# A hand-written engine order for an mLSTM layer and two gated MLPs: five loads and sigmoids of the output gates, and a new order of the first third

## The chip, the cores and the metric

The kernel runs on one core of one Trainium2 chip. The metric is the device time of one execution in microseconds (us), the median of several runs. The chip's engines work side by side and each in its own order: the tensor engine (PE), the vector engine (DVE), the scalar engine (ACT), GpSimd (POOL), and SP, whose queue issues nearly all the transfers (DMAs) here.

## The reference, cut to what matters

Inputs are q, k, v of 2 batches, 8 heads, 768 steps, 40 channels; an input, a forget and an output gate; and the weights of two MLPs of 320 x 1536, stored as 64-bit floats.

```python
m_new  = maximum(f + m, i);  f_stab = exp(f + m - m_new);  i_stab = exp(i - m_new)
C = f_stab * C + i_stab * outer(v_t, k_t);   n = f_stab * n + i_stab * k_t
y_t = sigmoid(o_t) * (C @ q_t) / maximum(abs(n @ q_t), 1)
x = y as (1536 tokens, 320)
x = (sigmoid(x @ w_gate) * (x @ w_val)) @ w_out
out = ((x @ w_a) * (x @ w_b)) @ w_out2
```

## The kernel before, in words

The recurrence is computed in 12 chunks of 64 steps, s = 0 to 11. Both MLPs work on 24 weight columns of 128 hidden channels (W0 to W11 of the first, W12 to W23 of the second), cut into units u = 0 to 83. Units 0 to 23 take two token blocks at a time (256 columns), the later ones four (512 columns).

What each engine does, and when, is written out by hand in PLAN (lines 67 to 127): a list of task names, in one order for all engines. Every engine takes its own tasks in the order of the list; a suffix :V, :G or :A says that the task goes to DVE, POOL or ACT. A suffix *n puts n matmuls of zeros (`fill`, line 171, which the profile shows as `first<-zb`) ahead of the task on PE. The tasks that the texts name, by chunk s, half p, gate chunk i, weight column c or unit u:

- `start`, `gl`i: loads of the gates (three chunks of 128, 320 and 320 steps). `ga`, `gb`, `gd`, `gc`i on DVE and `ge`i on ACT (lines 281 to 312) make the row V of cumulated gates from them. `cst` loads constants; `rhs`, `lhs`i copy them.
- `pr`s (line 341) puts V into the operands of `E`ps (PE, line 369), whose exponential `X`ps (ACT, line 378) is the decay matrix Dt. For s of 6 and more `pl`i does it with ten small DMAs.
- `kq`s, `kv`s load q, k and v. `yz`, `yi`i prepare the three buffers of v. `S`s (PE, lines 401 and 416) is k times q, `P`ps (DVE, line 426) multiplies it by Dt, `k`ps and `q`ps (lines 381 and 391) scale k and q by it. `ST`s (PE, line 435) and `st`s (ACT, line 457) update the state, `O`s (PE, line 445) makes the output.
- `og`i loads output gates (line 329, for the chunks named in OGS) and `sg`i takes their sigmoid on ACT (line 339). `N`s, `M`s, `D`s normalise; `T`s (PE) transposes; `xh`s (ACT, line 491) and `xl`s (DVE, line 494) write the high and low half of the MLP's input.
- `w`c loads a weight column (960 KB). `na`c (ACT, lines 218 and 219), `nb`, `ns`, `nc`c (DVE) and `nd`c (DVE, or POOL at about double the duration) narrow 64-bit floats to 32; `s1`c (ACT), `s2`, `s3`c (DVE or POOL) split them into two halves.
- `ma`u, `mb`u (PE, line 524) are a unit's first two products, `ga_`u (ACT), `gp`, `gm`u (DVE), `gh_`u (ACT), `gl_`u (DVE or POOL) its gate, and `mm`u (PE, lines 531 to 533) the product with w_out; `ev` adds it up.

ACT evaluates a function from a table that must be the one loaded. For u below 24 the gate is built of Exp, Tanh and Abs (line 535), which share the table of the Exp in `X`; the output gates' Sigmoid needs another one. The program starts with a Sigmoid on two elements (line 198).

```python
OGS = ((0, 2, 3), (2, 6, 3), (6, 12, 4))      # first chunk, last chunk + 1, weight buffer used
for entry in PLAN.split():
    ...
    if n and first is not None:
        fill(first, int(n))
    fn(eng.get(e))
```

Of the kernel before, what the change touches and what calls it, by code (L numbers as in the profile page):

```python
# [77 lines left out]
M5:V k06:G ma6 P07 gh_4 nb4 gl_4:G mb6 O6 ev1.3:A ga_5 P17 ns4 M4:V ev1.2:A k16:V ST6 gp5 gm5 nc4 ma7 D4 T4
ga_6 D5 T5 gh_5 q17:V gp6 gm6 gl_5:G mm4 xh4 xl4 mb7 xh5 xl5 mm5 ga_7 gh_6 nd4:G gp7 ev2.0 N6 s14 k07:G E08
X08 gl_6:G kq8 k17:V gm7 ma8 M6:V st6 w5 mb8 E18 X18 gh_7 ma9 kv8 gl_7:G E19 mb9 ga_8 q18:G ev2.1 mm6 mm7  # L80
q07:V O7 na5 kq9 gp8 ST7 S8 gm8 ga_9 ma10 mb10 ev3.3 ev3.2 N7 M7:V q08:G kv9 D7 nb5 gp9 ma11 gm9 gh_8 X19 E09
P18 gh_9 gl_9:V kv10 mb11 gl_8:G ga_10 gp10 mm8 st7 pl5 k18:G X09 D6 P08 T6 gm10 gh_10 T7 ns5 xh7 xh6 nc5
k08:G mm9 kq10 k19:V ga_11 xl6 O8 gp11 xl7 ST8 gm11 st8 S9 gl_10:G q19:G nd5:V N8 ma12 mm10 gh_11 E110 X110
mb12 ga_12 ma13 mb13 P09 k09:G s34:V P19 gp12 kq11 s15 gm12 gh_12 gl_11:V ga_13 M8:V ma14 s24:V gp13 D8 q09:G
E010 X010 O9 N9 M9:V gm13 ST9 mb14 s25:V mm11 gl_12:G ga_14 ev4.4:A ma15 gp14 gm14 D9 ev4.5:V gh_13 T8 xh8 xl8
T9 mb15 gl_13:G xh9 xl9 mm12 E111 ga_15 X111 q110:V gh_14 w6 ma16 k110:V gl_14:V mm13 mb16 gp15 gm15 ma17
k010:G mm14 na6 nb6 ga_16 E011 ns6 gp16 gh_15 mb17 nc6 ma18 st9 gl_15:V gm16 ga_17 s35:G w7 kv11 X011 nd6:V
gh_16 s16 mm15 gl_16:G S10 q111:G gp17 gm17 gh_17 S11 q010:V P010 ST10 st10 mb18 ga_18 P110 P111 q011:V P011
ev5.6:V gl_17:G O10 ev5.7:A O11 N10 M10:G mm16 mm17 N11 M11:V na7 D10 D11 T10 T11 gp18 gm18 xh10 gh_18 k111:G
nb7 xh11 xl11 xl10 ma19 mb19 ga_19 gp19 gl_18:G mm18 ns7 ma20 gm19 gh_19 mb20 ga_20 gp20 gm20 gh_20 s36:G ma21  # L90
gl_19:G nc7 mb21 ga_21 gp21 gm21 mm19 ma22 gl_20:G s26:V w8 mb22 ev6.8:A nd7:V ma23 ev6.9:A mm20 mb23 ga_22
gp22 gm22 gh_21 gl_21:G ga_23 gp23 ma24 gm23 s17 mm21 gh_22 mb24 gl_22:G gh_23 gl_23:G ga_24 s27:G k011:V mm22
na8 gm24 ma25 ma26 mb25 s37:G mm23 ga_25 w9 gh_24 mb26 ev7.11:V ev7.10:V gl_24 nb8 ga_26 ma27 ns8 nc8 mm24
gm25 nd8:V gh_25 mb27 gm26 gl_25 ga_27 mm25 na9 ma28 gh_26 gl_26 ma29 gm27 gh_27 ga_28 gl_27 mm26 nb9 ga_29
s18 ns9 nc9 mb28 nd9:V mm27 s38:V s19 s28:V ma30 w10 s29:G ev8.1 gm28 gh_28 mb29 gl_28 ev8.0 ga_30 s39:V ma31
w11 gm29 gh_29 gl_29 ma32 ev8.3 ga_31 na10 mb30 mb31 gm30 nb10 ev8.2 ma33 ns10 nc10 mm28 nd10:G mm29 gh_30
na11 gl_30 gm31 mm30 gh_31 ga_32 gl_31 mb32 s110 mm31 s210:G mb33 s310:G ev9.5 ev9.7 gm32 w12 ev9.4 gh_32 ma34
ga_33 gm33 gl_32 mb34 ev9.6 ga_34 nb11 gh_33 ns11 ma35 nc11 nd11:V mm32 s111 ma36 s211:V s311:G mb35 gl_33
ga_35 w13 mm33 gm35 gh_35 na12 gl_35 ma37 gm34 gh_34 mb36 gl_34 ga_36 mb37 ga_37 gm36 mm34 gm37 ma38 mm35 ma39
gh_36 ev10.11 gh_37 gl_36 ev10.9 ga_38 mb39 ev10.8 gl_37 ev10.10 ga_39 nb12 mb38 ns12 mm36 gm38 gm39 nc12 ma40  # L100
nd12:V mb40 na13 mm37 gh_38 nb13 ns13 ma41 gl_38 gh_39 s112 gl_39 nc13 mm38 ga_40 nd13:G ga_41 mm39 s312:G
mb41 ev11.0 gm40 ev11.1 s212:V ma42 gm41 w14 gh_41 mb42 gh_40 gl_40 gl_41 ga_42 ma43 gm42 ev11.2 ev11.3 yt1
# [831 lines left out]
```

## Time and profile before

| what | value |
|---|---|
| time, median of 3 runs | 476.27 us (474.78 to 476.99) |
| span of the profiled execution | 478.0 us; the page gives no other time for that execution |
| PE busy | 465.6 us, 97% of the span |
| DVE, ACT, POOL busy | 295.1, 242.5, 101.3 us |
| chain that ended last | PE 86%, DVE 6%, ACT 4%, DMA 2% |
| HBM read | 36.71 MB |
| loads, KB each | gates 64 and 160 (twice), cst 469, og 320, 640 and 960, kv twice 162, kq 512 |

The page's slices show PE full from end to end, DVE and ACT full in the first third and half idle later. Busy shares of PE are to be read with care here, since the matmuls of zeros count as busy, and so does a matmul at half the clock.

### The profile page before, as it was taken

The numbers are of one execution on the slowest core, as the hardware profiler recorded it, in microseconds if no ns is written. First come the engines' busy times: TensorE is split into PE (matmuls) and PEld (weight loads), VectorE is DVE, ScalarE is ACT, GpSimd is POOL, SyncE is SP. The second block draws the span as 40 slices with busy tenths as digits, with TensorE's granted clock in tenths as the row PEclk, the third lists the DMA queues.
The fourth block names the chain that finished last, engine by engine and source line by source line (L and its number), as shares of the span: only waits on it lengthen the run. The fifth ranks groups of instructions, "written<-read, shape, count | busy, mean of one in ns | idle before, by whom it ended". The sixth has DMA issues, their size and how long they took to land.

```text
span 478.0 us, 8676 instructions
## 1 busy us (share of the span) xinstructions
PE 465.6 (97%) x3511; PEld 406.2 (85%) x3516; DVE 295.1 (62%) x505; ACT 242.5 (51%) x455; POOL 101.3 (21%) x110
## 2 busy tenths in 40 slices
...
GB/s 226 309 201 240 86 180 224 32 103 183 1 84 84 1 166 0 83 84 1 33 49 84 7 160 0 1 82 138 28 84 82 1 83 1 0 1 20 36 55 55
DMA packets 10454, 39.31 MB, mean 82 GB/s; under 512 B 1840, under 2 KB 3760, under 8 KB 10416
## 3 DMA queue, kind: packets, MB, share of 16 engines
...
q8 instruction: 27, 0.44, 0.4%
...
HBM read 36.71 MB, written 1.97 MB: 81 GB/s over the span
## 4 chain that ended last, share of the span: by engine, by line
PE 86%; DVE 6%; ACT 4%; DMA 2%; issue 2%; SPq 0%; DVEq 0%
PE pa L524 30%; PE pb L524 23%; PE acc L531 8%; PE acc L532 8%; PE acc L533 8%; PE o L445 2%; PE sp L416 2%; DMA wst<-in_w_dram 2%; PE st L435 1%; ACT Dt L378 1%; PE e L371 1%; PE t L487 1%; DVE g L556 1%; PE tp L487 1%; PE first L174 1%
## 5 line engine op out<-in xcount | busy, mean ns | idle before, releaser
L524 PE MATMUL pa<-xb,W 128*128 128x512 f32 (+1 forms) x864 | 169.4, 343 | 0.3 <-DVE ge L605 0.3
L524 PEld LDWEIGHTS pa<-xb,W 128*128 128x128 f32 x864 | 136.3, 188 | 18.9 <-DVE ge L605 0.5
L524 PE MATMUL pb<-xb,W 128*128 128x512 f32 x480 | 119.0, 392 | 0.0
L524 PEld LDWEIGHTS pb<-xb,W 128*128 128x128 f32 x480 | 89.0, 188 | 17.9
L560 ACT ACTIVATE gh<-g 128x512 fp32r<-128x512 f32 (+1 forms) x84 | 47.5, 568 | 110.7 <-PE acc L532 55.6
L531 PE MATMUL acc<-W,gh 128*128 128x320 f32 x288 | 89.3, 310 | 0.0
L532 PE MATMUL acc<-W,gh 128*128 128x320 f32 x288 | 88.9, 309 | 0.0
L533 PE MATMUL acc<-W,gl 128*128 128x320 f32 x288 | 88.8, 309 | 0.0
L554 DVE TENSOR_TENSOR g<-g,pb 128x512 f32<-128x512 f32 x60 | 40.9, 685 | 69.7 <-PE pb L524 61.6
L565 DVE TENSOR_TENSOR gl<-g,gh 128x512 fp32r<-128x512 f32 (+1 forms) x66 | 45.5, 694 | 44.0 <-ACT gh L560 43.8
L549 ACT ACTIVATE g<-pa 128x512 f32<-128x512 f32 x60 | 35.6, 595 | 45.8 <-DVE gl L565 38.1
L532 PEld LDWEIGHTS acc<-W,gh 128*128 128x128 f32 x288 | 54.0, 188 | 2.1
L531 PEld LDWEIGHTS acc<-W,gh 128*128 128x128 f32 x288 | 54.0, 188 | 2.0
L533 PEld LDWEIGHTS acc<-W,gl 128*128 128x128 f32 x288 | 54.0, 188 | 0.0
L258 POOL TENSOR_TENSOR W<-wst,W 128x832 fp32r<-128x832 f32 x9 | 19.1, 2124 | 84.5 <-DVE x2tok L639 42.2
L639 DVE SCALAR_TENSOR_TENSOR x2tok<-acc,x2tok 128x320 f32<-128x320 f32 x52 | 23.8, 485 | 19.5 <-PE acc L533 19.5
L242 POOL TENSOR_TENSOR wst<-cva,wst 128x960 int32<-128x960 int32 x7 | 16.9, 2410 | 73.8 <-DVE cva L236 61.1
L218 ACT ACTIVATE cva<-wst 128x960 f32<-128x960 f32 x24 | 25.8, 1077 | 10.6 <-DVE wst L242 8.8
L252 ACT ACTIVATE W<-wst 128x832 fp32r<-128x832 f32 x24 | 23.2, 966 | 11.5 <-DVE wst L242 8.5
L236 DVE SCALAR_TENSOR_TENSOR cva<-wst,cva 128x960 int32<-128x960 int32 x24 | 27.9, 1161 | 0.4
L565 POOL TENSOR_TENSOR gl<-g,gh 128x256 fp32r<-128x256 f32 x18 | 15.7, 876 | 54.7 <-ACT gh L560 47.3
L219 ACT ACTIVATE wst<-wst 128x960 int32<-128x960 uint32 x24 | 26.1, 1087 | 0.0
...
## 6 DMA issues: line engine op xcount, KB each, us to landing
wst<-in_w_dram SPq DMA_DIRECT2D x24, 960.0 KB
...
og<-in_ogate_dram SPq DMA_DIRECT2D x1, 960.0 KB
...
rhsE<-V SPq DMA_DIRECT2D x24, 2.0 KB
```

The lines of the kernel that those rows point to most:

```text
L218: nc.scalar.activation(cva[0], hi.bitcast(F32), AF.Abs)
L219: nc.scalar.activation(lo, lo.bitcast(U32), AF.Copy, scale=2.0**-29)
L236: nc.vector.scalar_tensor_tensor(ai, hi, -0x40000000, ai, op0=ALU.bitwise_and, op1=ALU.bitwise_or)
L524: nc.tensor.matmul(dst, w[:, w0 : w0 + P], x[:, h, cb], start=(i == 0), stop=(i == 7))
L531: nc.tensor.matmul(a, gh[:, c], wh, start=st, stop=False)
L532: nc.tensor.matmul(a, gh[:, c], wl, start=False, stop=False)
L533: nc.tensor.matmul(a, gl[:, c], wh, start=False, stop=sp)
L549: nc.scalar.activation(t, pa, AF.Copy if l else AF.Sigmoid)
L554: nc.vector.tensor_tensor(t, t, pb, op=ALU.mult)
L560: nc.scalar.activation(gh, g, AF.Copy)
L565: eng.tensor_tensor(gl, g, gh.bitcast(F32), op=ALU.subtract)
L639: nc.vector.scalar_tensor_tensor(dst[:, 0:DM], acc, half, dst[:, 0:DM], op0=ALU.mult, op1=ALU.add)
```

## The change: what it does

Output gates come in five loads (chunks 0-1, 2-3, 4-5 into one buffer, 6-8, 9-11 into another) with five sigmoids. PLAN gets a new order up to the task `gl_21`; its last 682 entries are the same as before. The same tasks are on PE ahead of unit 24 as before. 64 matmuls of zeros become 33, and the 37 ahead of the first E become 2. Some 50 tasks change between DVE and POOL, and two evacuations between ACT and DVE. The load of W0 is issued after that of kq0, and its narrowing starts behind the first two exponentials.

```diff
-OGS = ((0, 2, 3), (2, 6, 3), (6, 12, 4))
+OGS = ((0, 2, 3), (2, 4, 3), (4, 6, 3), (6, 9, 4), (9, 12, 4))
...
-start gl1 cst rhs0:A lhs0:A ga0 ga1 gb0 gd0 ge0 lhs1:A w0 gb1 na0 gc0 gd1 ge1 pr0:V E00*37 og0 X00 rhs1:A
-pr1:V nb0 yz0 kv0 E01*1 E10*6 gl2 gc1 yz2 ns0 yz1 kv1 X01 X10 ga2 pr2:V yi0:A nc0 k10:V kq0 yi2:A k00:V E11*4
-X11 S0 pr3:V w1 kq1 E02 kq2 nd0:V E12 P10 P00 yi1:A k01:G kv2 ST0 st0 na1 X02 og2 S1*10 X12 k11:G k12:G og1
-kq3 gb2 gd2 O0 kv3 ST1 P11 P01 S2*2 pr4:V sg0 nb1 E03 s10 N0 O1*2 P02 P12 st1 s30:G k02:G kq4 ST2 sg2 N1 s20:V
-w2 E13 ns1 sg1 M0:G M1:V X03 nc1 k03:G D1 X13 k13:G O2*1 S3 P03 E04 P13 nd1:V E14 D0 kv4 X04 T0*1 X14 T1 st2
-xh0 N2 S4 ST3 xl0 pr5:G kq5 P14 xh1 kv5 xl1 O3 s11 s31:G s21:V P04 E15 ma0 N3 M2:V na2 mb0 k04:V ge2 ma1 M3:V
-ga_0 mb1 X15 S5 gp0 D3 k14:G st3 nb2 gm0 D2 T2 T3 ga_1 xh2 ns2 gc2 ST4 gh_0 gl_0:G nc2 xh3 O4 st4 kq6 xl2 xl3
...
+yz2 yz0 start ga0 gl1 gb0 ga1 cst gl2 gd0 ga2 lhs1:A rhs0:A ge0 og0 gc0 gb2 lhs0:A kq0 pr0:V w0 E10*2 rhs1:A
+sg0 yz1 gd2 gb1 X10 pr1:V kv0 E00 X00 S0*6 kq1 E11*2 gd1 E01*3 yi0:A k10:G P00 P10 kv1 na0 k00:G ST0*3 ge1 w1
+kq2 X11 X01 yi1:A nb0 st0 yi2:A gc1 ns0 pr2:V O0*1 ge2 nc0 S1 pr3:V kv2 nd0:V E12*3 E02 P11 P01 X02 X12 E13*8
+kq3 N0 gc2 S2 og2 k02:V k01:G k11:G kv3 og1 kq4 s10 pr4:V M0:V P12 og4 s30:G P02 X13 na1 kq5 O1*2 k12:G E04 N1
+nb1 E03 D0 X04 X03 ST1 st1 S3 T0*2 ST2 sg1 M1:V ns1 kv4 k03:G O2 k13:G P03 s20:V w2 nc1 P13 pl3 nd1:V st2 D1
+sg2 xh0 T1*1 N2 xl0 O3 S4 xh1 sg4 s11 E14 xl1 N3 pr5:G ST3 M2:G ma0 X14 k04:G P04 E15 s31:V s21:V P14 na2 mb0
+kv5 E05 X15 ga_0 M3:V D3 X05 D2 k14:V w3 nb2 ma1 ns2 S5 E16 X16 nc2 gp0 st3 nd2:V mb1 T2 kq6 T3 xh2 xl2 xh3
...
+gp3 gm3 gl_2:V M5:V S7 S6 k06:V q07:V P06 kv7 s13 st5 P16 mb4 P17 ST6 og3 na4 D5 mm2
+ga_4 gh_3 T5 s23:G s33:V sg3 xh5 ma5 gp4 gm4 nb4 O6 pl4 ma6 k07:V gh_4 gl_3:V mb5 M4:G st6 D4 mm3 ga_5 q17:G
...
-        ogw[k] = wpool.tile([P, 2 * NH + 2 * P], F32, tag=f"W{k}", name=f"og{k}"), s0
+        ogw[k] = wpool.tile([P, 2 * NH + 2 * P], F32, tag=f"W{k}", name=f"og{k}"), min(o[0] for o in OGS if o[2] == k)
```

## Rows read from the trace of the kernel before

**Rows 1.** Windows by stage: length, busy us of PE, PEld, DVE, ACT, POOL, PEclk, DMA share, GB/s.
```profile
7.00:27.50 20.50, 17.00 (x205) 9.51 (x205) 18.95 (x36) 18.19 (x30) 3.14 (x3) 1.00 1.03 316
27.50:37.60 10.10, 9.35 (x125) 6.88 (x129) 4.68 (x13) 6.78 (x9) 3.31 (x6) 0.50 0.39 98
45.40:103.04 57.64, 56.61 (x808) 53.62 (x806) 52.95 (x102) 47.13 (x111) 23.80 (x24) 1.00 0.43 137
103.04:139.86 36.82, 36.82 (x460) 35.91 (x460) 31.41 (x61) 26.45 (x68) 12.91 (x17) 1.00 0.23 75
139.86:474.00 334.14, 332.75 (x1736) 291.99 (x1734) 177.07 (x273) 135.68 (x225) 51.14 (x49) 1.00 0.15 51
```

**Rows 2.** Timeline of ACT: start, length, line, what, idle before it.
```profile
10.38 1.08 ACT L218 ACTIVATE cva<-wst 128x960 f32<-128x960 f32 x1 [1.66 <-DMA wst<-in_w_dram]
14.71 0.60 ACT L378 ACTIVATE Dt<-e 128x512 f32<-128x512 f32 x1
15.20 1.05 ACT L682 ACTIVATE rhsE<-cs 128x1024 fp32r<-128x1024 f32 x1
...
24.04 1.09 ACT L378 ACTIVATE Dt<-e 128x512 f32<-128x512 f32 x2
25.14 1.28 ACT L339 ACT_TABLE_LOAD   x1
26.44 0.74 ACT L339 ACTIVATE x2tok<-og 128x640 f32<-128x640 f32 x1
```

**Rows 3.** Timeline of PE, matmuls of zeros in two windows, and the first E.
```profile
1.17 5.73 PE L174 MATMUL first<-zb 128*128 128x512 bf16 x13 [1.17 <-DVE zb L178]
7.32 4.70 PE L174 MATMUL first<-zb 128*128 128x512 bf16 x21
11.88 0.58 PE L371 MATMUL e<-rhsE,lhsE 128*128 128x512 f32 x1
```

**Rows 4.** Chain that ended last, in order of time: start, us, what.
```profile
26.02 1.49 issue
...
29.11 0.31 PE sp L401
...
31.52 0.72 PE e L371
...
33.12 1.87 PE o L445 x32
34.99 1.09 PE st L435 x32
...
45.56 3.77 PE pa L524 x32
49.33 0.21 PE sp L401
...
50.69 0.81 PE tp L487 x6
51.50 0.74 PE st L435 x32
52.24 0.93 PE o L445 x32
53.17 0.43 PE e L371
```

**Rows 5.** One window from the first gate load to the second `xl`, columns as in Rows 1.
```profile
3.31:44.65 41.34, 36.55 (x497) 23.28 (x502) 32.25 (x65) 31.02 (x51) 9.99 (x14) 0.88 0.87 261
```

**Rows 6.** Timeline of DVE, the end of `pr0` and the second `xl`.
```profile
10.77 0.28 DVE L351 TENSOR_TENSOR lhsE<-V,cs 32x128 fp32r<-32x128 f32 x1
...
44.10 0.55 DVE L494 TENSOR_TENSOR xb<-tp,xb 128x384 fp32r<-128x384 f32 x1
```

**Rows 7.** The page's DMA issues: KB each.
```profile
wst<-in_w_dram SPq DMA_DIRECT2D x24, 960.0 KB
```

**Rows 8.** Timeline of SP, eight of the ten issues of `pl3`.
```profile
50.60 5.72 SPq L364 DMA_DIRECT2D rhsE<-V  x8
```

More of the change, by code (lines that the diff above doesn't have):

```diff
@@ L73 @@
-xh0 N2 S4 ST3 xl0 pr5:G kq5 P14 xh1 kv5 xl1 O3 s11 s31:G s21:V P04 E15 ma0 N3 M2:V na2 mb0 k04:V ge2 ma1 M3:V
-ga_0 mb1 X15 S5 gp0 D3 k14:G st3 nb2 gm0 D2 T2 T3 ga_1 xh2 ns2 gc2 ST4 gh_0 gl_0:G nc2 xh3 O4 st4 kq6 xl2 xl3
-nd2:V w3 E05 X05 ma2 mb2 s12 gp1 gm1 pl3 ga_2 ma3 P15 P05 gh_1 k05:G na3 mb3 s22:V gl_1:V s32:V mm0 mm1 kq7
-gp2 ma4 mb4 E06 E07 w4 gm2 ga_3 ev0.0:A ev0.1:A nb3 ns3 nc3 nd3:V X06 gh_2 k15:G X07 N4 kv6 S6 gp3 gm3 kv7 E16
-s13 P06 ST5 gl_2:G X16 P16 gh_3 gl_3:V O5 pl4 ga_4 S7 st5 E17 mm2 s23:V s33:G gp4 gm4 N5 mm3 X17 ma5 mb5 na4
@@ L78 @@
[L78 to L102, printed above, removed]
@@ L103 @@
-ma44 yh1 ga_43 yl1 na14 mm40 nb14 mm41 ns14 nc14 yt0 mb43 nd14:V yh0 gh_42 s113 yl0 gl_42 ma45 gm43 ga_44
-s213:G s114 mm42 gh_43 s313:V gl_43 mb45 w15 ga_45 mb44 gm45 mm43 gm44 gh_44 yt3 yt2 ev12.4 ma46 yh3 yh2 yl3
-gh_45 yl2 na15 gl_44 mb46 gl_45 ev12.6 ga_46 ma47 gm46 nb15 s314:V mb47 ns15 ga_47 nc15 ma48 ev12.5 nd15:V
+yz2 yz0 start ga0 gl1 gb0 ga1 cst gl2 gd0 ga2 lhs1:A rhs0:A ge0 og0 gc0 gb2 lhs0:A kq0 pr0:V w0 E10*2 rhs1:A
+sg0 yz1 gd2 gb1 X10 pr1:V kv0 E00 X00 S0*6 kq1 E11*2 gd1 E01*3 yi0:A k10:G P00 P10 kv1 na0 k00:G ST0*3 ge1 w1
@@ new lines @@
+ST4 xl3 O4 ma2 E06 E17 gm0 s12 k05:V kq7 mb2 ga_1 gh_0 P05 P15 k15:G st4 na3 gp1 ma3 gm1 gl_0:V gh_1 N4 nb3
+ga_2 O5 kq9 X06 ST5 gl_1:V X17 mm0 mb3 ns3 gp2 gm2 E07 gh_2 ga_3 mm1 nc3 nd3:V s22:G kv6 ev0.1:A ev0.0:A gp3
+N5 s32:G w4 k16:G ma4 X07 gm3 gl_2:V M5:V S7 S6 k06:V q07:V P06 kv7 s13 st5 P16 mb4 P17 ST6 og3 na4 D5 mm2
+ga_4 gh_3 T5 s23:G s33:V sg3 xh5 ma5 gp4 gm4 nb4 O6 pl4 ma6 k07:V gh_4 gl_3:V mb5 M4:G st6 D4 mm3 ga_5 q17:G
+mb6 P07 T4 ns4 xl5 gl_4:V nc4 ev1.2:V E18 gp5 O7 k17:V ev1.3:A xh4 xl4 gm5 mm4 nd4:V N6 ma7 E08 X18 ga_6 gp6
@@ new lines @@
+X08 gh_5 E19 kq8 gm6 X19 mb7 gl_5:V ga_7 gh_6 M6:V S8 gl_6:G w5 kv8 q19:V P18 mm5 N7 gp7 D6 na5 gm7 M7:G ev2.1
+P08 ma8 T6 mb8 ga_8 xh6 kv9 ev2.0 ma9 gp8 xl6 ST7 E09 mb9 X09 gh_7 gl_7:G mm6 S9 D7 s14 gm8 k18:G ga_9 gh_8
+st7 q18:V ma10 nb5 T7 xh7 k08:G P19 kq10 q08:V mm7 ST8 ev3.2 xl7 gp9 P09 k09:V gm9 ev3.3 pl5 s24:V st8 q09:G
+O8 gl_8:G mb10 E011 N8 ga_10 gp10 kq11 gh_9 mm8 s34:G kv10 gm10 ma11 E010 gl_9:G k19:G O9 X011 M8:G gh_10 N9
+ns5 M9:V X010 gl_10:V mb11 E110 E111 ga_11 D8 gp11 nc5 mm9 ma12 X111 X110 w6 ST9 mb12 q110:V gm11 nd5:V S10
@@ new lines @@
+ma13 P010 ga_12 kv11 D9 gh_11 gp12 k110:G P110 gm12 k010:V q010:G q011:G gl_11:G st9 na6 mm10 T9 T8 ma14 mb13
+ST10 gh_12 gl_12:G ga_13 gp13 xh8 mm11 xh9 mb14 ma15 xl9 gm13 nb6 gh_13 gl_13:G xl8 ev4.5:V ga_14 ev4.4:A s15
+O10 ns6 gp14 N10 mb15 mm12 ma16 nc6 gm14 gh_14 s35:V gl_14:G ga_15 nd6:V q111:G S11 mm13 gp15 mb16 st10 ma17
+mm14 gm15 M10:V ga_16 D10 T10 P011 P111 gh_15 gl_15:G gp16 gm16 s25:V mb17 xh10 gh_16 ga_17 s16 O11 N11 ma18
+gl_16:V M11:V k111:V mm15 mb18 gp17 D11 gm17 ev5.7:A ev5.6:A ma19 T11 w7 xl10 mm16 ga_18 gp18 xh11 gm18 xl11
@@ new lines @@
+gh_17 gh_18 gl_17:G mb19 ga_19 s26:G gp19 gl_18:V na7 s36:V ma20 mm17 mb20 gm19 ma21 mm18 ga_20 gh_19 mb21
+gp20 ma22 nb7 gm20 w8 gl_19:V mm19 gh_20 ns7 gl_20:V ga_21 gp21 gm21 mb22 nc7 ma23 gh_21 ev6.8:A ev6.9:A ga_22
+gp22 mm20 gm22 nd7:V mb23 gl_21:G ga_23 gp23 ma24 gm23 s17 mm21 gh_22 mb24 gl_22:G gh_23 gl_23:G ga_24 s27:G
+k011:V mm22 na8 gm24 ma25 ma26 mb25 s37:G mm23 ga_25 w9 gh_24 mb26 ev7.11:V ev7.10:V gl_24 nb8 ga_26 ma27 ns8
+nc8 mm24 gm25 nd8:V gh_25 mb27 gm26 gl_25 ga_27 mm25 na9 ma28 gh_26 gl_26 ma29 gm27 gh_27 ga_28 gl_27 mm26 nb9
```

11 lines of the change are left out of this document (added).

## The prediction, made before the changed kernel was run

> **What bounds the kernel now.** I first read the windows by stage. From the first product of unit 0 at 45.4 us, PE is idle for 1.0 of 57.6 us, then for none of 36.8, then for 1.4 of 334 us, at the full clock (1.00, which is 2.4 GHz) [rows 1]. The change leaves the work and the order behind unit 24 alone. So the end comes earlier only as far as the start of unit 0 (`ma0`, at 45.56 in the chain [rows 4]) comes earlier and the stage behind it stays as dense.
>
> Second, what sets 45.4. Up to the second `xl`, in the 41.3 us from 3.31 on, DVE is busy for 32.25 us [rows 5]. It waits most between 27.5 and 37.6 us: 4.68 of 10.10 us busy, with PE at a granted clock of 0.50, its 1.2 GHz level [rows 1]. There the chain of waits runs along PE: an idle stretch of 1.49 us at 26.0, then S, O and ST at the lower level [rows 4]. At its start the timeline of ACT shows the other delay. ACT waits 1.66 us for W0, narrows it, and evaluates the first exponential only at 14.71, although its E was issued at 11.88 [rows 2, 3]. So PE and DVE bound the first 45 us in turns, and the later stages are PE's.
>
> **Part 1: W0 after kq0, its narrowing behind X10 and X00.** ACT's old order put the narrowing of W0 ahead of X00. In the new one ACT has, from the 8.72 us at which it went idle [rows 2], one `rhs` copy (1.05 us), the first sigmoid (0.74) and a table load (1.28), which ends at 11.8 [rows 2]. DVE swaps `gb1` and `gd1` ahead of pr0 for `ga2` and `gb2`, about equal work, so pr0 ends at 11.05 as before [rows 6]. Two E at the lower clock (0.72 each [rows 4]) make X10 start at 11.8 and X00 end at 13.0, where X00 alone ended at 15.3 and X10 came after it. kq0 becomes the sixth load; gates, constants, og0 and kq0 are 1685 KB, as much as stood up to W0 before (1653 KB), and W0 was there at 10.38 [rows 2]. W0 and its 960 KB [rows 7] now end 992 KB further on, at 316 GB/s [rows 1] 3.1 us later, at 13.5. ACT reaches it at about 13.9, behind the copy `yi0`, so the later landing costs nothing. If that cover is gone, ge1 and X11 wait as long as W0 is late. On SP nothing is queued behind the later W0 but kv0 and kq1, which have over 3 us to spare. Behind kq3, which waits until P00 and P10 have read kq0 (about 19 us), stand og2, kv3, og1 and kq4, all needed after 25 us. `pl3`, whose first eight issues took 5.72 us [rows 8], now stands ahead of kv5 and w3 on SP; both are wanted some 10 us later, and w3 waits for the split of W1 behind unit 0 anyway. k00 and k10 go to POOL, which was busy for 3.1 of 20.5 us [rows 1], and are done before PE comes to ST0.
>
> **Part 2: zeros, 64 to 33.** Thirteen zeros took 5.73 us from a cold start (0.44 us each), 21 later ones 4.70 (0.22) [rows 3]: the engine had run 5.7 us of back-to-back zeros before the spacing halved. Taking away 35 ahead of the first E frees no time, since X00 waited for ACT. It has a price: E10 now finds PE at the lower level. From 11.0 us on PE has up to `ma0`: 31 zeros, 10 E, 5 S, 4 ST, 4 O, two T. At the full clock these are 31 x 0.22 + 10 x 0.43 + 5 x 1.36 (the S from 49.33 to 50.69) + 4 x 0.74 + 4 x 0.93 + 0.81 = 25.4 us [rows 3, 4]. At the lower one they are 31 x 0.44 + 10 x 0.72 + 5 x 2.41 (29.11 to 31.52) + 4 x 1.09 + 4 x 1.87 + 1.6 (estimated as twice 0.81) = 46.4 us [rows 3, 4]. With H us spent at the lower level PE is ready for `ma0` at 11.0 + 25.4 + 0.453 x H. H is not shown by any row; its bounds are 0 and the whole stretch. I take 6.5, the E, the six zeros and S0 from 11.0 to 17.5, near the 5.7 of the zeros: PE is ready at 39.3.
>
> **Part 3: DVE's order.** Up to the second `xl` the new list has gc2, k02 and M0 more and k00, k10 and P14 less, a wash within 0.3 us, so DVE's work stays 32.2 us. Without any wait it would end at 35.5, with all of the old waits at 44.6. At the share of the stretch from 7 to 27.5 (18.95 of 20.50 [rows 1]) it takes 34.8 us and ends at 38.1. S0, which P00 needs, ends at 17.5, 1.7 us after DVE has come to P00 at about 15.8; added in full that gives 39.8. I take the middle, 39.0. `ma0` stood 0.75 us behind the end of that `xl` (45.40 against 44.65 [rows 6]), so it starts at 39.75, behind PE's 39.3. **Gain: 45.4 - 39.75 = 5.65 us**, between 0 and 9.0 (36.4, PE without any lower clock).
>
> **Part 4: sigmoids and table loads.** The first sigmoid finds its table loaded by the program's start, but the others now come in two batches, `sg1` `sg2` `sg4` and, after unit 0, `sg3`. Each batch needs a load of the Sigmoid's table and one back. After `xh1` ACT now has sg4 (about 1.0 us, from 0.74 for two chunks), a table load (1.28) and X14 (0.6) ahead of the first `ga_`, less ge2 (1.0), which is done before. Around there ACT has no idle to hide them, so this delays the first gate by 1.9 us. sg3 and its two table loads (about 3.6 us) fall into the stage where ACT is busy 47.1 of 57.6 us [rows 1]; 52 of 57.6 still fit. The added DVE work of the moves (about +1.4 us net by this trace's durations, 52.95 of 57.64 busy before) fits too. I take 1.9 us as given back, between 0 (PE has E15, E05, ma1, S5 and E16 to go on with) and 5.5, all of it exposed. The extra og loads cost SP two issues and move no more bytes.
>
> One rule of the Trainium skill speaks against this part. The row first: X's pair ends at 25.13, the table load starts at 25.14 and lasts 1.28, the sigmoid starts at 26.44 [rows 2], so 1.28 is all that the switch cost here. The Trainium skill (ScalarE: Activation LUTs, "What ACT_TABLE_LOAD costs") states 1.28 us for the load and another 1.38 us for emptying the engine, 2.66 in all. By that figure the first gate would be late by 3.3 instead of 1.9 us.
>
> **Sum:** -5.65 + 1.9 = -3.75 us. The profiled execution's 478.0 us, 1.7 above the median, becomes 474.25; put on the median of 476.27 it is **472.5 us**. About 0.5% (2.4 us) is what a measurement can tell from no change.
>
> **The rivals.**
> - *ACT and DVE give it all back.* Unit 0 starts earlier, but the stage behind it, where DVE is 92% busy and ACT rises from 82 to 90%, stretches by the 5.5 us of the bound. For it: the chain runs through DVE and ACT there. Against it: both start that stage earlier as well, with the same work done. 476.27 - 5.65 + 5.5 = 476.1. Chance 0.22.
> - *The cold clock decides.* Without the early zeros PE stays at 1.2 GHz, or falls back in a gap, as at 26 us after an idle of 1.49 us [rows 4]. The place is S0 to S2. The gain is gone when `ma0` reaches 43.5, at H = 15.7, and from H = 21 the kernel is slower by over 0.5%. At H = 30 `ma0` is at 50.0, and the time is 476.27 + 4.6 + 1.9 = 482.8. For it: between 27.5 and 37.6 PE was 93% busy and still got only 0.50 [rows 1]. Against it: zeros stand ahead of S0, E11, E01 and ST0 one after the other. Chance 0.13. The Trainium skill (TensorE: Matmul & The Clock Gate, "What's actually happening") says that throttled is the default and that activity releases it; by that rule the first E of the new kernel run at half rate, and the zeros of the kernel before agree.
> - *Each switch of table also drains ACT.* ACT would then stop for 1.4 us more at a table load (an estimate from the Trainium skill's page named above); with 1.4 us more ahead of the first gate and two more switches for sg3, 0 to 2.8 exposed, the gain shrinks to 2.35 or less: 473.9 to 476.7. The row shows no such stop. Chance 0.03.
> - *The change does not bite:* kq0 or og0 lands late, ACT stands as long as it stood for W0, X10 begins after 14.7 as X00 did. Then the front keeps its 45.4: 476.3. Chance 0.02.
>
> **How the numbers follow.** My case has 0.60: faster by over 0.5% in 0.58 and within it in 0.02. Its own range is 467.3 (9.0 us gained, nothing given back) to 473.8 (H of 10.1, as long as the stretch at 0.50 was: `ma0` at 41.0). The gate stage adds 0.20 to no change and 0.02 to slower; the clock 0.02 and 0.11; the last two 0.05 to no change. So faster 0.58, same 0.29, slower 0.13. The range runs from 467.5 up to 478.5, which is the front's gain gone with the 1.9 us still paid (478.2); beyond it lies only most of the clock's case and the end of the best one.
>
> **What would show it.** Right: X10 at about 12 us; the first S near 15 to 17, with a granted rate of half until about 17 and full from then to 39; DVE idle for under 5 us between 3.3 and the second `xl`; `ma0` between 38.5 and 41; four table loads by `ga_0` and two around sg3; later stages as dense as now, and unit 24 some 4 us before 139.9. Wrong: `ma0` later than 43.5; a stretch at 0.50 of over 16 us in all; PE idle for more than 3 us between unit 0 and unit 24, with ACT or DVE as releaser; X10 still waiting for a load.

## The result, and the profile after

The changed kernel takes 481.3 us (median of 6 runs, 479.87 to 482.08) against 476.88 us of the kernel before beside it (6 runs, 474.78 to 479.58). The ratio is 1.0102, with a 95% interval of 1.007 to 1.0135: about 1% slower. The forecast was 472.5 us and faster, so size and sign both failed.

First the windows by stage of the kernel after (columns as in [rows 1]).

```profile
7.00:27.50 20.50, 15.43 (x203) 9.22 (x207) 19.57 (x36) 19.03 (x33) 5.32 (x7) 1.00 1.03 314
27.50:39.00 11.50, 8.75 (x210) 6.94 (x211) 11.46 (x19) 9.24 (x16) 5.40 (x5) 0.99 0.58 187
39.00:45.60 6.60, 6.58 (x80) 5.69 (x79) 5.78 (x16) 4.83 (x7) 1.66 (x3) 0.50 0.25 85
43.32:145.15 101.83, 99.51 (x1284) 93.99 (x1281) 86.01 (x167) 79.79 (x187) 35.26 (x35) 0.99 0.37 119
145.15:476.00 330.85, 330.04 (x1722) 289.59 (x1720) 175.85 (x270) 133.24 (x219) 51.22 (x49) 1.00 0.15 49
3.31:40.45 37.14, 25.63 (x441) 17.61 (x447) 35.44 (x66) 29.62 (x51) 12.16 (x14) 0.98 0.88 270
```

`ma0` starts at 43.32, and unit 24's second product (the first `pb` of 512 columns, where the order is the old one again) at 145.15. So the stage between them takes 101.83 us. From 27.50 to 39.00 DVE is busy for 11.46 of 11.50 us and PE for only 8.75. The clock is full where it was at 0.50 before [rows 1], and at 0.50 later, from 39.00 to 45.60.

The same views of a second execution of the kernel before, taken beside the experiments, followed by the row of its `ma0`.

```profile
27.50:37.60 10.10, 8.68 (x218) 7.05 (x217) 7.86 (x18) 9.75 (x14) 4.12 (x7) 1.00 0.69 190
42.83:139.22 96.39, 96.10 (x1281) 91.94 (x1279) 85.07 (x167) 76.40 (x184) 37.22 (x41) 1.00 0.39 120
139.22:471.00 331.78, 330.04 (x1722) 289.78 (x1720) 175.84 (x270) 133.20 (x219) 51.19 (x49) 1.00 0.15 50
3.31:40.45 37.14, 30.76 (x440) 19.44 (x444) 30.57 (x58) 29.45 (x47) 10.22 (x13) 0.95 0.93 270
```

```profile
42.83 1.40 PE L524 MATMUL pa<-xb,W 128*128 128x256 f32 x10
```

This execution has no stretch at 0.50 between 27.5 and 37.6 (it has a shorter one, from 17.5 to 20.9), and its `ma0` is at 42.83, not at the 45.40 on which the prediction stood. Its stage up to unit 24 takes 96.39 us, with 0.29 us of PE idle. In the first execution the same stage takes 97.17 us:

```profile
45.40:142.57 97.17, 96.14 (x1280) 91.91 (x1279) 85.61 (x166) 76.02 (x184) 36.71 (x41) 1.00 0.36 116
```

After the change that stage takes 101.83, with 2.32 us of PE idle. Behind unit 24 PE's work is the same: it is busy for 330.04 us and makes 1722 matmuls in both last windows. So the loss, 4.7 to 5.4 us, lies between `ma0` and unit 24, and the front gave nothing back for it. Of the 5.4 us against the second execution, 2.0 are idle time of PE, some 0.3 are E15, which the new list moves behind `ma0`, and about 1 is the first eight products of unit 0 at half the clock (2.08 us, against 1.18 in `new_to_mm1`). The other 2 us are time in which PE counts as busy; no row shows what makes them.

ACT after the change (start, length, line, what, idle before it):

```profile
7.11 0.63 ACT L682 ACTIVATE lhsE<-cs 128x512 fp32r<-128x512 f32 x1 [4.90 <-DMA cs<-in_cst_dram]
...
10.69 0.72 ACT L339 ACTIVATE x2tok<-og 128x640 f32<-128x640 f32 x1
11.43 1.28 ACT L378 ACT_TABLE_LOAD   x1
12.73 1.08 ACT L378 ACTIVATE Dt<-e 128x512 f32<-128x512 f32 x2
...
14.67 1.10 ACT L218 ACTIVATE cva<-wst 128x960 f32<-128x960 f32 x1
...
42.22 1.28 ACT L378 ACT_TABLE_LOAD   x1 [1.63 <-PE e L371]
```

The first exponentials run at 12.73, and W0's narrowing at 14.67 waits for nothing.

PE (the same columns):

```profile
11.69 1.22 PE L371 MATMUL e<-rhsE,lhsE 128*128 128x512 f32 x2 [9.49 <-DVE lhsE L351]
12.72 2.57 PE L174 MATMUL first<-zb 128*128 128x512 bf16 x6
15.21 0.65 PE L401 MATMUL sp<-kq,cs 40*64 40x512 f32 x2
...
15.74 0.90 PE L416 MATMUL sp<-kq 40*64 40x64 f32 x16
...
37.97 1.05 PE L445 MATMUL o<-Y,Z 128*64 128x41 f32 x28 [1.79 <-DVE Z L426]
...
43.32 2.08 PE L524 MATMUL pa<-xb,W 128*128 128x256 f32 x8
...
66.81 0.90 PE L435 MATMUL st<-Y,Kw 128*40 128x41 f32 x32 [1.24 <-DVE Kw L381]
68.33 0.41 PE L531 MATMUL acc<-W,gh 128*128 128x320 f32 x1 [0.62 <-DVE Z L426]
```

At O3 PE stands (is idle and waits) 1.79 us for DVE's P13; at ST6 and `mm2` it stands 1.24 and 0.62 us for k06 and the P tasks.

DVE, and then POOL beside it:

```profile
19.56 1.22 DVE L345 TENSOR_TENSOR rhsE<-V,cs 32x512 fp32r<-32x512 f32 x1
20.79 0.73 DVE L351 TENSOR_TENSOR lhsE<-V,cs 32x128 fp32r<-32x128 f32 x1
...
22.63 0.67 DVE L345 TENSOR_TENSOR rhsE<-V,cs 32x512 fp32r<-32x512 f32 x1
23.32 0.28 DVE L351 TENSOR_TENSOR lhsE<-V,cs 32x128 fp32r<-32x128 f32 x1
...
31.83 1.03 DVE L477 SCALAR_TENSOR_TENSOR xt<-nrm,xt 128x320 f32<-128x320 f32 x1
32.78 1.19 DVE L230 TENSOR_SCALAR cva<-cva 128x960 int32<-128x960 int32 x1
33.89 0.68 DVE L426 TENSOR_TENSOR Z<-sp,Dt 128x512 f32<-128x512 f32 x1
...
39.49 0.96 DVE L494 TENSOR_TENSOR xb<-tp,xb 128x384 fp32r<-128x384 f32 x2
...
51.81 1.02 DVE L494 TENSOR_TENSOR xb<-tp,xb 128x384 fp32r<-128x384 f32 x2 [2.10 <-ACT xb L491]
...
63.85 2.30 DVE L477 SCALAR_TENSOR_TENSOR xt<-nrm,xt 128x320 f32<-128x320 f32 x1
```

```profile
19.38 2.00 POOL L381 TENSOR_TENSOR Kw<-Y,Dt 128x320 f32<-128x320 f32 x2 [2.04 <-ACT Y L574]
...
31.58 1.88 POOL L381 TENSOR_TENSOR Kw<-Y,Dt 128x320 f32<-128x320 f32 x2 [3.33 <-ACT Dt L378]
33.41 1.69 POOL L345 TENSOR_TENSOR rhsE<-V,cs 32x512 fp32r<-32x512 f32 x1
...
63.76 2.05 POOL L258 TENSOR_TENSOR W<-wst,W 128x832 fp32r<-128x832 f32 x1 [5.55 <-ACT W L252]
```

The same instruction of DVE is short alone and long beside POOL: `rhsE` 0.67 us at 22.63 and 1.22 at 19.56, with POOL busy from 19.38 to 21.38; `lhsE` 0.28 and 0.73; `xt` 2.30 at 63.85, with POOL busy from 63.76 to 65.81. The product of P at 33.89, which reads `sp` from the matmul's output, keeps its 0.68 beside POOL.

### The profile page after: what moved, and what is told of

Read it like the earlier page. It is cut to its first block, busy times and chain, and to the rows that moved or that the text cites. A ratio compares the mean times of both kernels' runs of the same rounds, so it can differ in the third digit from the quotient of the medians.

```text
span 480.0 us, 8632 instructions
## 1 busy us (share of the span) xinstructions
PE 459.1 (96%) x3480; PEld 403.3 (84%) x3485; DVE 300.7 (63%) x512; ACT 245.4 (51%) x459; POOL 102.4 (21%) x105
## 3 DMA queue, kind: packets, MB, share of 16 engines
q1 hardware_dynamic: 10416, 38.45, 24.8%
## 4 chain that ended last, share of the span: by engine, by line
PE 88%; DVE 5%; issue 2%; ACT 2%; DMA 1%; POOL 1%; SPq 0%; POOLq 0%; DVEq 0%
PE pa L524 32%; PE pb L524 23%; PE acc L531 9%; PE acc L533 9%; PE acc L532 9%; PE o L445 2%; PE sp L416 2%; DMA cs<-in_cst_dram 1%; DVE Z L426 1%; PE st L435 1%; PE e L371 1%; PE t L487 1%; PE tp L487 1%; POOL Z L391 1%; DVE rhsE L345 1%
## 5 line engine op out<-in xcount | busy, mean ns | idle before, releaser
L524 PE MATMUL pa<-xb,W 128*128 128x512 f32 (+1 forms) x864 | 172.9, 346 | 0.0
L524 PEld LDWEIGHTS pa<-xb,W 128*128 128x128 f32 x864 | 138.1, 189 | 18.7
L565 DVE TENSOR_TENSOR gl<-g,gh 128x512 fp32r<-128x512 f32 (+1 forms) x71 | 48.4, 686 | 44.8 <-ACT gh L560 44.6
L258 POOL TENSOR_TENSOR W<-wst,W 128x832 fp32r<-128x832 f32 x12 | 25.5, 2127 | 94.5 <-ACT W L252 43.5
L242 POOL TENSOR_TENSOR wst<-cva,wst 128x960 int32<-128x960 int32 x6 | 14.3, 2392 | 73.8 <-DVE cva L236 61.1
L242 DVE CUSTOM_DVE_ANT_0 wst<-wst,cva 128x1920 uint16<-128x1920 uint16 x18 | 22.6, 1254 | 0.6
```

The costliest lines, as they stand in the source:

```text
L242: e.tensor_tensor(lo, cva[0].bitcast(I32), lo, op=ALU.add)
L524: nc.tensor.matmul(dst, w[:, w0 : w0 + P], x[:, h, cb], start=(i == 0), stop=(i == 7))
L565: eng.tensor_tensor(gl, g, gh.bitcast(F32), op=ALU.subtract)
```

## The experiments

Seventeen kernels were run, the kernel before and the changed one again among them. "Stage" is the time from `ma0` to unit 24's second product, read from PE's rows of the one profiled execution of each (96.4 in the second execution of before, 101.8 after).

**The kernel before again.** No edit.

> The kernel before, profiled once more. Its first profile (478.0 us span, 27.5 to 37.6 us at a granted clock of 0.50) stood above most of its timed runs, whose median is 476.9. If that stretch at half the clock is an accident of one execution, this profile has a shorter one or none, unit 0 starts at 42 to 43.5 us instead of 45.4, and the span is 474.5 to 476. If it belongs to the kernel, unit 0 starts at 45 to 46 us again and the span is 477 to 478.5.

Measured: 475.88 us, ratio 0.9991 (0.995 to 1.0031), `ma0` at 42.83. The first profile's 45.40 is not what this kernel does each time. The mean granted clock of that first execution was 0.986; of the 105 other runs of the kernel before whose clock is on record, only 2 have one as low.

**Front and rest apart.** `front_new_rest_old` takes the new list up to `ma0` (with og3 and sg3 directly behind og4 and sg4) and the old list's order of everything left; `front_old_rest_new` the reverse.

```diff
-... ST3 M2:G ma0 X14 k04:G P04 E15 s31:V s21:V P14 na2 mb0 kv5 ...
+... ST3 M2:G ma0 X14 P14 kv5 s31:G s21:V P04 E15 na2 mb0 k04:V ma1 M3:V ga_0 ...
```

> The new order up to unit 0's first product (with sg3 drawn in behind sg4, so that there is one batch of late sigmoids), then the old order of all that is left, with the old split between DVE, POOL and ACT. If the loss sits in the new order behind unit 0 (DVE and POOL in each other's way, two more table loads), this kernel loses it and keeps what the front gained: 474 to 477 us. If the loss sits in the front (the clock that falls to half ahead of unit 0, cold start without the 37 zeros), it stays at 480 to 482 us.

> The old order up to unit 0's first product with the three old sigmoids, then the new order of what is left. If the loss sits behind unit 0: 480 to 484 us, as slow as the changed kernel or slower. If it sits in the front: 475 to 478 us, as fast as the kernel before.

Measured: `front_new_rest_old` 477.31 us, ratio 1.0024 (0.9996 to 1.0052), `ma0` at 42.93, stage 97.3. This is just above the 474 to 477 us expected. The new front alone neither gains nor clearly loses; by this, the larger part of the loss lies in the new order behind it. `front_old_rest_new` took 488.01 us, 1.0234 (1.0159 to 1.031), but its time says nothing of the parts, since the mixed list made a wait that neither kernel has, for the small transfers of `pl`:

```profile
53.57 0.77 PE L370 MATMUL e<-rhsE,lhsE 128*128 128x512 f32 x1 [3.74 <-DMA lhsE<-V]
```

Its old front is one more look at `ma0` in the old order: 45.12 us, behind a stretch at 0.50 from 35.2 to 45.4.

**PE kept busy ahead of O3.**

```diff
-N2 xl0 O3 S4 xh1
+N2 xl0 O3*9 S4 xh1
```

> The changed kernel with nine matmuls of zeros ahead of O3, to fill the 1.8 us in which PE waits for P13 and after which the granted clock falls to 0.50 from 38.9 to 45.6 us. If that fall is what the change lost, the clock stays at 1.00, S4, ST3 and unit 0's first products take half their time, and the time falls by 2.5 to 3.5 us to about 478 us. If the stage behind unit 0 is bound by DVE and ACT anyway, unit 0 starts up to 1.5 us earlier but the time moves by less than 1 us.

> The new order up to unit 0 with nine zeros ahead of O3, and the old order behind it. With the zeros unit 0 started at 40.7 us in the changed kernel, and the old order behind unit 0 took 97.3 us with the new front. If both add up, unit 24's second product comes at 138 us, 1.2 us before that of the kernel before, and the time is 474 to 475.5. If the old stage is held by DVE and ACT as well, the earlier start is lost in it and the time is 476 to 477.5.

Measured: with the whole new list (`o3_zeros`) 480.26 us, ratio 1.0093 (1.006 to 1.0126). `ma0` comes at 40.73 in this execution, 2.6 us earlier, and the stage grows to 102.9. The windows and the row of ST6 show where it goes:

```profile
38.00:46.00 8.00, 7.91 (x142) 7.02 (x139) 7.89 (x19) 7.31 (x13) 1.66 (x3) 1.00 0.43 128
...
62.00:70.00 8.00, 5.70 (x75) 5.20 (x77) 7.76 (x14) 7.84 (x15) 3.53 (x4) 0.79 0.45 142
```

```profile
63.68 0.90 PE L435 MATMUL st<-Y,Kw 128*40 128x41 f32 x32 [1.74 <-DVE Kw L381]
```

The clock is full up to `ma0`, but PE then stands 1.74 us at ST6 instead of 1.24, and the clock falls there (0.79 from 62 to 70). DVE did not get earlier, so PE only waits later. In the other three profiled kernels with these zeros `ma0` is at 41.86 to 42.53, so not all of the 2.6 us is theirs. With the old rest behind the same front (`front_new_zeros_rest_old`) it is 476.02 us, 1.0012 (0.9991 to 1.0032): a tie with the kernel before, and as good as any version tried.

**The sigmoids of the last chunks, the split on POOL, the old engines.** Three edits of the whole new list.

```diff
-og4 ... sg4 ... ST6 og3 ... s33:V sg3
+og4 og3 ... sg4 sg3 ... ST6 ... s33:V
-T5 s23:G s33:V
+T5 s23:V s33:V
```

The third, `engines_old`, gives the tasks that changed between DVE and POOL or ACT their old engines (51 in the list that ran).

> The changed kernel with the load og3 behind og4 and the sigmoid sg3 behind sg4, so that the two table loads and the sigmoid in mid-stage (3.6 us of ACT) become 1.0 us ahead of unit 0. If the table loads are a main part of the 5.4 us that the stage from unit 0 to unit 24 grew by, the time falls by 2 to 3.5 us to 478 to 479. If they lie in ACT's idle time, as forecast, it stays within 1 us: 480.5 to 482.

> The changed kernel with one task put back from POOL to DVE: s23, the subtraction that ran on POOL for 2.05 us while DVE's M5 beside it took 2.30 us instead of 0.49, ahead of PE's idle 2.4 us at 65.6 to 68.3. If POOL slows DVE down and that gap is on the path to the end: M5 is back at 0.5, the gap falls under 1 us, the time by 1 to 2.4 us, to 479 to 480.3. If DVE is simply short of time there, its 0.95 us for s23 take the place of the stretch and the time stays within 0.7 us.

> The new order with the old engine for every task that both orders have (52 tasks back to where they were on DVE, POOL or ACT). If the new split between DVE and POOL is what costs, the time falls by 3 us or more, to 478 or less. If it is the order itself, with units and attention dealt in another sequence, it stays at 480 to 484 us, since the split had been fitted to the order.

Measured: `sg3_early` 481.76 us, ratio 1.0137 (1.0097 to 1.0178); `s23_on_dve` 481.38, 1.0131 (1.0098 to 1.0163); `engines_old` 485.6, 1.0221 (1.0187 to 1.0256). So sg3 and its two table loads cost nothing that can be measured, and the old engines on the new order are worse, with PE standing for a split of the weights on DVE:

```profile
61.75 0.50 PE L524 MATMUL pa<-xb,W 128*128 128x256 f32 x2 [2.68 <-DVE W L258]
```

Ahead of `ma0`, though, `engines_old` is the better kernel. With k00 and k10 back on DVE, POOL has no task from 4.1 to 24.8 us, and the `rhsE` and `lhsE` that took 1.22 and 0.73 us beside it are short (DVE's rows, then PE's):

```profile
19.80 0.67 DVE L345 TENSOR_TENSOR rhsE<-V,cs 32x512 fp32r<-32x512 f32 x1
20.49 0.28 DVE L351 TENSOR_TENSOR lhsE<-V,cs 32x128 fp32r<-32x128 f32 x1
```

```profile
36.80 1.02 PE L445 MATMUL o<-Y,Z 128*64 128x41 f32 x28 [0.87 <-DVE Z L426]
...
40.86 2.07 PE L524 MATMUL pa<-xb,W 128*128 128x256 f32 x8
```

Its `ma0` comes at 40.86; in the eleven profiles with the changed front on its new engines and no zeros ahead of O3 (some with og3 and sg3 moved up) it comes at 42.09 to 43.69. Its stage behind, 107.7 us, is by far the longest.

In `s23_on_dve` the `xt` product that took 2.30 us is short again, since POOL no longer splits weights beside it. It brought no time, and PE still stands at ST6, now released by ACT:

```profile
64.61 0.49 DVE L477 SCALAR_TENSOR_TENSOR xt<-nrm,xt 128x320 f32<-128x320 f32 x1
```

```profile
65.75 0.90 PE L435 MATMUL st<-Y,Kw 128*40 128x41 f32 x32 [1.06 <-ACT Y L457]
```

**Where in the new order.** The new list up to a task X, and from there the old list's order of what is left (sg3 early, kq9 in its old place): X is `mm1`, some 15 us behind `ma0`, `mm2`, some 25, or `ga_7`, some 40. The theory then was that the loss sits at ST6 and `mm2`, where the new list deals S7, S6, ST6 and DVE's share of them ahead of `mm2`. `st6_behind_ma5` tests it in another way:

```diff
-M5:V S7 S6 k06:V q07:V P06 kv7 s13 st5 P16 mb4 P17 ST6 og3 na4 D5 mm2 ... nb4 O6
+M5:V S7 S6 P06 kv7 s13 st5 P16 mb4 P17 og3 na4 D5 k06:V q07:V mm2 ... nb4 ST6 O6
```

> The new list up to mm1 (some 15 us behind the start of unit 0), from there on the old list's order of what is left; all five gates' sigmoids in their early places, og3 and sg3 directly behind og4 and sg4. Theory (the loss sits where the new list deals S7, S6, ST6 and their DVE work ahead of mm2, 20 to 30 us behind unit 0): that place has the old order here, so 477 to 478.5 us, a ratio of 1.000 to 1.005, and a stage from unit 0 to unit 24 of 97 to 98.5 us. Rival 1 (the loss is made in the first 15 us behind unit 0, by the fall of the clock and DVE's stretched work): 480 to 481.5 us. Rival 2 (it is spread over the whole stage): 479 to 480.

> The new list up to mm2 (some 26 us behind the start of unit 0), so with S7, S6, ST6, k06, q07, P06, P16 and P17 ahead of mm2, then the old list's order of what is left. Theory: the loss is all in by then, 480 to 481.5 us, a stage of 100.5 to 102 us. Rival 1 (made before mm1): also 480 to 481.5, but then new_to_mm1 shows it too. Rival 2 (spread): 479.5 to 480.5. If the early attention buys work that the later part needs less of, 478 to 479.

> new_to_mm2 with nine matmuls of zeros ahead of O3, so that PE does not stand idle there. If the fall of the clock costs 2.5 us by itself, every run has a clock of 0.997 or more and 477.0 to 477.8 us. If DVE is what bounds the stretch up to mm2 (as the kernel after the change with these zeros showed, which gave most of it back at ST6), 479 to 480 us, and a wait of PE for DVE of over 1.5 us between unit 0 and mm2.

> The new list up to ga_7 (some 40 us behind the start of unit 0), then the old list's order of what is left. If the loss is spread, it lies between new_to_mm2 and the kernel after the change: 479.5 to 481 us, 478.5 to 479.3 in runs at a full clock. If all is lost up to mm2, the same as new_to_mm2 (477.4 at a full clock). If the loss lies in the end of the new order, behind ga_7, also as new_to_mm2.

> The kernel after the change with k06 and q07 behind D5 on DVE and ST6 behind ma5 on PE, all else as in it. Theory (PE stands for DVE's k06 at ST6 and then for P17 at mm2): both waits lose their releaser, 1.5 to 2.5 us come back, 478.8 to 479.8 us. Rival (DVE's total work bounds this stretch, so the wait only moves to ma5, O6 or mm3): 480.8 to 481.5 us, with a wait of PE on DVE or POOL of over 1 us within the next 10 us.

> The changed kernel again, unedited. If the fall of the clock behind O3 is a matter of the single execution, its runs fall into two groups by their mean granted clock, near 0.992 and near 1.000, 1.5 to 2.5 us apart (481.3 and 479.5); if the clock costs nothing beyond what DVE costs anyway, the groups are under 0.7 us apart.

Measured: 

| kernel | median us | ratio (95% interval) | stage |
|---|---|---|---|
| `new_to_mm1` | 478.35 | 1.0042 (1.0015 to 1.0069) | 98.9 |
| `new_to_mm2` | 479.77 | 1.004 (1.0012 to 1.0068) | 100.8 |
| `new_to_mm2_zeros` (O3*9) | 477.94 | 1.0047 (1.0022 to 1.0072) | 99.3 |
| `new_to_ga_7` | 480.59 | 1.0092 (1.0059 to 1.0124) | 101.3 |
| `st6_behind_ma5` | 481.67 | 1.01 (1.0064 to 1.0137) | 101.8 |
| `after_again` | 481.86 | 1.012 (1.0059 to 1.0181) | 101.9 |

The theory fell twice. A part of the loss is there at `mm1`, before the place in question, the cut behind `mm2` adds little to it, and the cut at `ga_7` adds more. And with ST6 put later PE stands as long at the next task that needs DVE:

```profile
65.13 0.41 PE L531 MATMUL acc<-W,gh 128*128 128x320 f32 x1 [1.80 <-DVE Z L426]
```

The runs of one kernel differ in their mean granted clock. Those of the changed kernel lie at 0.993 and below or at 0.997 and above; those of the kernel before lie anywhere from 0.986 to 1.000. Traces of `new_to_mm1` and `new_to_mm2`, whose lists are the same up to `mm1`, show one place where they part (the row of O3 on PE and a window around it, of the first and then of the second):

```profile
38.66 1.01 PE L445 MATMUL o<-Y,Z 128*64 128x41 f32 x28 [1.00 <-DVE Z L426]
```

```profile
38.00:46.00 8.00, 7.34 (x139) 6.64 (x143) 7.92 (x20) 7.82 (x12) 1.97 (x4) 1.00 0.38 136
```

```profile
37.67 1.02 PE L445 MATMUL o<-Y,Z 128*64 128x41 f32 x28 [1.79 <-DVE Z L426]
```

```profile
38.00:46.00 8.00, 8.00 (x110) 7.15 (x107) 7.60 (x18) 6.52 (x9) 1.66 (x3) 0.60 0.42 141
```

Where PE stood 1.00 us at O3 the clock stayed at 1.00; where it stood 1.79 it fell to half. The length of this stand alone does not decide it: in `engines_old` PE stood 0.87 us at O3, and the clock was at 0.50 from 39.4 to 42.7. Sorted by clock, the medians in us, with the number of runs:

| kernel | 0.996 or more | below 0.996 |
|---|---|---|
| before, all runs beside the experiments and `before_again` | 474.9 (52) | 477.1 (53) |
| `front_new_zeros_rest_old` | 476.0 (10) | none |
| `front_new_rest_old` | 476.3 (3) | 477.4 (7) |
| `new_to_mm1` | 477.9 (5) | 479.5 (5) |
| `new_to_mm2` | 477.4 (3) | 479.9 (7) |
| `new_to_mm2_zeros` | 477.9 (10) | none |
| `new_to_ga_7` | 478.9 (4) | 481.1 (6) |
| `o3_zeros` | 480.2 (5) | 480.3 (5) |
| after (both sets) | 479.7 (2) | 481.5 (8) |

So the runs with the lower clock are 1.1 to 2.5 us slower, in the kernel before as well; `o3_zeros`, where the profiled execution has its fall only at ST6, shows no difference. At either clock the change costs about the same, 479.7 - 474.9 = 4.8 and 481.5 - 477.1 = 4.4 us. And the loss grows with the length of the new list. Against the kernel before in the same set of runs and on the same side of 0.996, it is 0.6 to 1.4 us with the new front alone, 1.1 to 3.0 with the new list up to `mm1` or `mm2`, 4.0 up to `ga_7`, and 4.6 to 5.5 for the whole list (`after_again`). Steps of under 1 us, and groups of 1 to 4 runs, are at the edge of what these runs tell apart; that the loss is spread is what they show.

**DVE's stand at xl2.** In the new list DVE stands 2.10 us for `xh2` (the row at 51.81). Two edits: `t2_early` moves T2, T3 and what follows from them ahead of S5; `xl2_late` fills the stand with work that is ready.

```diff
-ma1 ns2 S5 E16 X16 nc2 gp0 st3 nd2:V mb1 T2 kq6 T3 xh2 xl2 xh3 ST4 xl3
+ns2 ma1 T2 T3 xh2 xl2 xh3 xl3 S5 E16 X16 nc2 gp0 st3 nd2:V mb1 kq6 ST4
-mb1 T2 kq6 T3 xh2 xl2 xh3 ST4 xl3 O4 ma2 E06 E17 gm0 s12 k05:V kq7 mb2 ga_1 gh_0 P05 P15
+mb1 T2 kq6 T3 gm0 k05:V P05 P15 xh2 xl2 xh3 ST4 xl3 O4 ma2 E06 E17 s12 kq7 mb2 ga_1 gh_0
```

> The kernel after the change with T2, T3, xh2, xh3, xl2 and xl3 ahead of S5 and E16. If DVE's shortage up to mm2 makes the wait at ST6, of which its own wait of 2.1 us for xh2 is the largest part, the wait of PE at ST6 and mm2 falls below 0.7 us and the time by 1.5 to 2 us, to 479.3 to 480. If DVE then only waits elsewhere, 481 to 481.6 as before.

> The kernel after the change with gm0, k05, P05 and P15 on DVE ahead of xl2, where DVE stood for 2.10 us. Theory (DVE's shortage makes the wait at ST6 and mm2, and that wait is time of the whole): the stand at xl2 falls below 0.7 us, PE's waits at ST6 and mm2 from 1.86 us together to below 0.6, and the time by 1.3 to 2 us, to 479.5 to 480.2. Rival (PE only waits later, at ma5, O6 or mm3, or ACT's xh2 and gates are late instead): 481 to 482.

> The same with nine matmuls of zeros ahead of O3. Theory: both losses are gone, a full clock from O3 to mm2, waits of PE up to mm2 of less than 1.5 us in all, 477.5 to 478.8 us. Rival: what the zeros give is lost again at ST6, as without the edit on DVE: 480 to 481 us.

Measured: `t2_early` 482.43 us, ratio 1.0143 (1.0088 to 1.0199); its edit missed, since the stand became longer:

```profile
49.85 1.02 DVE L494 TENSOR_TENSOR xb<-tp,xb 128x384 fp32r<-128x384 f32 x2 [3.49 <-ACT xb L491]
```

`xl2_late` did take that stand away, and took 481.54 us, 1.0099 (1.0062 to 1.0136). DVE stood for ACT's gate instead, and PE at ST6 as long as before:

```profile
54.59 0.42 DVE L605 SCALAR_TENSOR_TENSOR ge<-ge,pa 128x256 f32<-128x256 f32 x1 [1.46 <-ACT g L538]
```

```profile
67.10 0.90 PE L435 MATMUL st<-Y,Kw 128*40 128x41 f32 x32 [1.25 <-DVE Kw L381]
```

With the zeros ahead of O3 as well (`xl2_late_zeros`) it was 479.49 us, 1.0059 (1.0025 to 1.0093), between theory and rival. The engines hand the delay round: what is filled on DVE is waited for on ACT, and what PE gains at the start it loses at ST6. None of the versions beats the kernel before.

## Why the prediction was wrong, point by point

In short, both terms of the sum failed. The gain of 5.65 us at the front was counted from 45.4 down to 39.75; `ma0` came at 43.32, against 42.83 in the second execution of the kernel before, so there was no gain. The 1.9 us given back in the stage behind became 4.7 to 5.4.

- **What bounds the kernel.** The reading of the last stage held. Its 45.4 us for `ma0` came from one execution, with a stretch at 0.50 [rows 1] that the second execution does not have; there `ma0` is at 42.83. So 2.6 of the 5.65 us could be had only in executions with so long a stretch. Such executions exist (`front_old_rest_new`, with the same old front, has its `ma0` at 45.12), but by the mean clock, 0.986 and as low in only 2 of 105 other runs, the profiled one is no usual one. This is the first step that failed.
- **Part 1** held nearly. X10 and X00 end at 13.81 instead of 13.0, since the constants came later (ACT stood 4.90 us up to 7.11) and pr0 ended at 11.64 instead of 11.05. kq0 was in time for S0 at 15.21, and W0 cost nothing. k00 and k10 on POOL made PE wait for nothing; their cost was in DVE, below.
- **Part 2.** The start was better than taken: the two E and six zeros run at the lower rate (2.57 us for six), but S0 from 15.21 to 16.57 already takes 1.36, the full rate. That is 3.5 us, not 6.5. The clock fell later, behind the stand at O3, from 38.8 to 45.65; 4.5 us of that lie ahead of `ma0`. Together H is 8.0, for which the prediction's formula gives 40.0; PE's waits, as the 1.79 us for DVE at O3, are not in it.
- **Part 3** failed in its term for DVE's work. "DVE's work stays 32.2 us" became 35.44 us, with 12.16 us of POOL beside it, against 32.25 and 9.99 [rows 5]. The exchange of tasks was the wash that the prediction took it for (64 instructions in both, 0.14 us less by their durations before); the instructions were longer, 3.2 us in sum, beside a POOL that had k00, k10 and M2 in place of k02 and M0. DVE's waits were 1.7 us where the prediction had 3.5. So its second `xl` ends at 40.45 instead of 39.0. P13 is late, PE stands 1.79 us and the clock falls. With PE at half the clock, `ma0` starts 2.87 us behind that `xl` and not 0.75, the other part of the delay. In the kernels with zeros ahead of O3, where the clock stays full, `ma0` comes at 40.73 to 42.53, still 1 to 2.8 us behind the predicted 39.75. The rows on POOL and DVE bear out the Trainium skill (SBUF — State Buffer, "Who interferes with whom"), by which a DVE instruction with two SBUF inputs contends with a GpSimd instruction that reads SBUF; the product of P, with one input from PSUM, was not stretched. The row at 32.78, a TENSOR_SCALAR on a single tensor, was long too (1.19 us, against 0.65 in the kernel before), and that sentence does not cover it. Three such pairs were undone: `xt` fell from 2.30 to 0.49 us when POOL's split went away, and `rhsE` and `lhsE` from 1.22 and 0.73 to 0.67 and 0.28 when k00 and k10 did. That all of the 3.2 us comes from this is read from the rows; in `engines_old` DVE's work up to the second `xl` still is 34.6 us, with other instructions stretched.
- **Part 4** was right on sg3: `sg3_early` changed nothing. The table load ahead of X14 was not hidden: ACT stood 1.63 us for E14 and made the load only then, so X14 came 1.28 us later, and DVE stood 0.54 us for it at 44.15. The first gate came 3.46 us behind `ma0` (at 46.78), against 2.51 (at 45.34) in the second execution of the kernel before: 0.95 us for the 1.9 of the sum. How much of it is the load's was not tested. No stop besides the 1.28 us is seen: the sigmoid at 10.69 ends at 11.41, the load ends at 12.71 and the exponential starts at 12.73. So the Trainium skill's further 1.38 us (ScalarE: Activation LUTs, "What ACT_TABLE_LOAD costs") is again not in the trace.
- **That the stage behind stays as dense** was the premise that cost most. The stage was 4.7 to 5.4 us longer where the sum had 1.9, near the 5.5 of the rival by which ACT and DVE give all back; with no gain of the front to set against it, this is the slower kernel. That rival named the right place, but not the right size of what stood against it. None of the signs that the prediction named for being wrong came about: `ma0` was not later than 43.5, PE stood 2.3 and not over 3 us, the stretches at 0.50 stayed under 16 us, and X10 waited for no transfer. It had no sign for a stage that takes longer while PE counts as busy. The runs show that the loss grows along the new order. They do not show which dealing of tasks makes which part of it: three edits that took one wait away moved it, and this stays open.
- **The clock's rival** saw a fall in a gap; it came at O3, not from S0 to S2. It delays `ma0`, but the kernel before loses as much in the runs in which its clock falls, so it is not what parts the two kernels.
